# One piece of w_in over two DMA queues, the first scores in other PSUM banks, and other counts of filler products, in a recurrent-attention and shrink kernel

## The chip, the core and the metric

The kernel runs on one core of one Trainium2 chip. The metric is the time of one execution on the device in microseconds (us), as a median over executions. The core has a matrix engine (PE, with its weight loads shown as PEld), a vector engine (DVE), a scalar engine (ACT), a general engine (POOL), and a sync engine (SP) that here only issues DMA transfers. ACT can issue transfers too. Every engine works through its own list of instructions strictly in the order in which they were written; engines meet through semaphores only.

## The reference

Four batches, eight heads, 768 steps, head size 48. A state of 48 x 48 per head decays and is updated at each step, and the attention's output feeds a two-layer block with the activation h - tanh(h):

```
for t in range(S):
    state = alpha[:, :, t, :, None] * state + einsum('bhd,bhe->bhde', k[:, :, t], v[:, :, t])
    y[:, :, t] = einsum('bhd,bhde->bhe', q[:, :, t], state)
x = y.transpose(0, 2, 1, 3).reshape(3072, 384)
h = x @ w_in                      # 384 x 2048
out = (h - tanh(h)) @ w_out       # 2048 x 384
```

The weights arrive as 64-bit floats, all else as 32-bit floats.

## The kernel before

**Tiling.** The 3072 tokens are worked in 12 units (u) of 256, each of two chunks (c) of 128. For each unit the recurrence is done in chunk form: alpha, k and q are turned so that head dimensions lie on partitions, running products of alpha are made by scans forwards (`W`) and backwards (`U`), k and q are scaled with them (`kT`, `qT`), a product of the two gives the scores of a chunk, these are masked (`pm`), and the output y is the masked scores times v plus q times the state. The result `xT` goes through 8 steps (s) of the two-layer block: `first u:s` (six products with w_in, line 1080), `square` and `quad` on ACT (lines 1089 and 1093), `cube` and `shrunk` on DVE (1097 and 1101), `second u:s` (products with w_out, line 1125 for units 0 and 1, line 1146 after them).

**Weights.** w_in and w_out come in eight pieces each, `in0` to `in7` and `out0` to `out7`. A piece is fetched by `load_weight` (lines 39 to 44): a piece of w_in as eight transfers of 96 KB (six of 48 rows, two of 16), a piece of w_out as one. All are issued by SP. Each is then read by two ACT instructions (lines 86 and 87) and finished by two on DVE (lines 89 and 90). There are four raw buffers, so the fetch of a piece waits until the piece four before it was read.

**The start.** For unit 0, alpha, k, q and v are loaded in two halves each, one half issued by SP and one by ACT (lines 584 and 595). PE turns them by products with an identity matrix (`turn`, line 663): alpha's two parities a and b into the PSUM banks `o0` and `o1`, k's into the two `h` banks, q's into the large tile `sc`. ACT and DVE copy alpha out (line 670). DVE then makes U and W for each chunk and multiplies k and q out of PSUM (line 679). The scores of chunk 0 stand in tile `sc` as well, those of chunk 1 in the `h` banks (lines 782 to 800). `sc` exists once, so the scores of chunk 0 can only be written when all four multiplications of q have read it. Then come `masked` (819), `back` (925, k turned back), `natural` (930, its copy by ACT), `update` (938), `state` (953, 955), `gaps` (830, 833, small copies by ACT), `y` (850 to 860) and `x` (911, 920: ACT copies y into `xT`). `first 0:0` needs `x` of both chunks and in0 finished.

**The order.** A planner (class `Planner`) holds tasks with an engine, an estimated duration, dependences and a latency, lists them by an estimated schedule, and the program is written in that order. Its estimates set only the order of instructions on the engines; nothing waits for them on the chip. Two of its settings matter here. `plan.begin` is when it thinks that an engine starts. `plan.filler` puts products of the identity with itself (`spin`, line 1208) into PE's list, one for every 0.35 us of a gap that the plan leaves on PE before `y 0.0`; nobody reads their result. The filler is written into PE's list, so PE works it off whether or not there is a gap.

**DMA semaphores.** Transfers take eight semaphores in turn, in the program's order across both issuing engines. The program's instructions show the consequence: every issue from the ninth on first waits until the transfer that last held its semaphore has landed. While it waits, nothing behind it on its engine runs.

Of the kernel before, what the change touches and what calls it, by code (L numbers as in the profile page):

```python
# [9 lines left out]
FP32 = mybir.dt.float32  # L10
# [7 lines left out]
P = 128  # L18
# [17 lines left out]
R_MAX = 2.0 ** 60  # L36


def load_weight(nc, pool, rows, **kw):

    raw = pool.tile([P, WN], I64 if rows[0][2].dtype != FP32 else FP32, name="raw", **kw)
    for at, js, src in rows:
        nc.sync.dma_start(out=raw[at].rearrange("p (j n) -> p j n", n=src.shape[-1])[:, js], in_=src)
    return raw


# [275 lines left out]
class Planner:  # L322
# [64 lines left out]
    def order(self):  # L387
        names = {t[0]: i for i, t in enumerate(self.tasks)}
        assert len(names) == len(self.tasks)
        before, after = ([[] for _ in self.tasks] for _ in range(2))  # L390
        for i, t in enumerate(self.tasks):
            edges = {names[a]: self.tasks[names[a]][6] for a in t[4]}
            if t[7]:
                edges.setdefault(names[t[7]], 0.0 if self.tasks[names[t[7]]][1] == t[1] else 0.25)
            for j, lat in edges.items():
                before[i].append((j, lat))
                after[j].append((i, lat))
        chance = random.Random(self.SEED)
# [12 lines left out]
        plan = sorted(((starts[i], n, self.tasks[i][5], i) for n, i in enumerate(order)), key=lambda x: x[:2])  # L411

        engine, until, us, do = self.filler
        filled, free = [], self.begin.get(engine, 0.0)
        for x in plan:
            name, e, length = self.tasks[x[3]][:3]
            if e == engine and until:
                filled += [(free, -1, do, None)] * int(max(0.0, x[0] - free) / us)
                free = x[0] + length
                until = until if name != until else None  # L420
            filled.append(x)
        return filled


def fast(tc, q, k, v, alpha, moe_w_in, moe_w_out, out, w_in, w_out, ident, ok, pad_rows):
    nc = tc.nc
    B, H, S, D = q.shape
    NP = H // 2
# [9 lines left out]
    PLAIN = 2  # L438
# [4 lines left out]
    with ExitStack() as ctx:  # L443
# [23 lines left out]
        def by_matmul(u, what):  # L467
            return u < len(TURNED) and what in TURNED[u]
# [80 lines left out]
        raw_of = {}  # L549

        def fetch(what, s):
            raw_of[what, s] = load_weight(nc, raw_pool, weight_parts(moe_w_in, moe_w_out, pad_rows, what, s), bufs=4)

        def convert(what, s):
            it = []
# [7 lines left out]
        for n, (what, s) in enumerate(pieces):  # L563
            rank = RANK[what] + 2 * s
            held = pieces[n - 4] if n >= 4 else None
            add(f"fetch {what}{s}", "SP", 5.7 if n < 2 else 4.3 if what == "in" else 2.0, rank - 30, [held and f"read {held[0]}{held[1]}"],
                lambda what=what, s=s: fetch(what, s), lat=2.5)
# [35 lines left out]
        def gla(u, rank):  # L603
# [17 lines left out]
            for what, name in enumerate(("aT", "kT", "qT", "v")):  # L621
                go(f"load {name}", "SP", 1.3 if direct or what == 3 or by_matmul(u, what) else 2.2, -9 + 0.1 * what,
                   [what < 3 and u > 0 and not by_matmul(u - 1, what) and not by_matmul(u, what) and f"{name}{prev}"]
                   + [u == 1 and ("kUba 0" if what == 3 else "turn qTb 0")]
                   + [f"{last} {u - 2}.{CU - 1}" for last in ("y", "state") if what == 3 and u > 1
                      and (last == "y" or (u - 2) % UPB < UPB - 1)],
                   lambda what=what: load(u, what), lat=2.9 if u == 0 else 3.6 if u < PLAIN else 4.5)

            def widen(what):
                for hh in range(2):  # L630
# [51 lines left out]
            for n, ab in enumerate("ab"):  # L682
# [87 lines left out]
            def chunk(c):  # L770
# [11 lines left out]
                def scores():  # L782
                    if c == 0:

                        xT[u] = two.tile([P, NP, TU], FP32, name="xT")
                    if u == 0 and c == 1:
                        sc = m["sc", c] = [ps_h.tile([P, 2, TU], FP32, name="h").rearrange(
                            "p a t -> p (a t)").rearrange("p (g t) -> p g t", t=P) for _ in range(2)]
# [25 lines left out]
                def masked():  # L814
                    sc = m["sc", c]
                    if direct:
                        m["pm", c] = [two.tile([P, NP, P], FP32, name=f"pm{r}", tag=tag) for r, tag in enumerate("zw")]
                        for r, to in enumerate(m["pm", c]):
                            V.tensor_mul(to, sc[r] if c else sc[:, r], mask.unsqueeze(1).to_broadcast([P, NP, P]))
# [384 lines left out]
        def spin():  # L1204
# [1 line left out]
            if not spun:  # L1206
                spun.append(ps_o.tile([P, P], FP32, name="spin", tag="o2"))
            T.matmul(spun[0], lhsT=ident, rhs=ident, start=True, stop=True)  # L1208
# [113 lines left out]
```

## Time and profile before

| what | value |
|---|---|
| four executions | 575.84, 576.33, 580.06, 576.11 us |
| median | 576.22 us |
| the profiled execution's own time | 575.63 us |
| its span, first to last instruction | 573.9 us (1.73 us lie around it) |
| mean granted PE clock | 0.995 |
| PE, DVE, ACT busy | 98%, 79%, 56% |
| instructions | 13746 |

The page of the profile gives, for each engine, its busy time and count; PE's count has two entries for each 32-bit product, and one for each transpose. A busy PE is not yet a PE at its peak, because a product's end is modelled. What counts in the following is therefore the distance from the start of one group of products to the start of the next. A timeline row has the start, the length and the engine, then source line, operation, tiles and count; in square brackets stands the idle time just before it and what ended it. A table by windows gives the busy time of each engine in a stretch, the PE clock that was granted (1.00 is full), the share of the DMA engines in use and GB/s.

Where PE's first 55 us go, by the starts of its groups in the timeline: fillers from 1.57, alpha's turning from 5.39, the other turnings to 10.78, fillers, `back` and `update` to 14.1, nothing to 16.36, scores from 16.36, y from 20.87, the turnings of unit 1 from 25.60, `first 0:0` from 28.32, `y 1.1` up to 54.28. From 54.28 on `first` and `second` follow each other at 2.59 and 2.58 us, then 2.59 and 2.27.

### The profile page before, as it was taken

The numbers are of one execution on the slowest core, as the hardware profiler recorded it, in microseconds if no ns is written. First come the engines' busy times: TensorE is split into PE (matmuls) and PEld (weight loads), VectorE is DVE, ScalarE is ACT, GpSimd is POOL, SyncE is SP. The second block draws the span as 40 slices with busy tenths as digits, with TensorE's granted clock in tenths as the row PEclk, the third lists the DMA queues.
The fourth block names the chain that finished last, engine by engine and source line by source line (L and its number), as shares of the span: only waits on it lengthen the run. The fifth ranks groups of instructions, "written<-read, shape, count | busy, mean of one in ns | idle before, by whom it ended". The sixth has DMA issues, their size and how long they took to land.

```text
span 573.9 us, 13746 instructions
## 1 busy us (share of the span) xinstructions
PE 563.1 (98%) x5583; PEld 497.7 (87%) x5583; DVE 450.7 (79%) x886; ACT 323.4 (56%) x559; POOL 4.8 (1%) x22
## 2 busy tenths in 40 slices
PE   8899999999999999999999999999999999999995
PEld 8777777778999989998998999899898999899995
DVE  6888889999999996896895895896797745544643
ACT  3699895647687775676584374364353433333530
POOL 3000000000000000000000000000000000000000
PEclk9899999999999999999999999999999999999999
DMA  8889871335664762562630320310200000000001
GB/s 179 206 243 249 263 155 52 88 85 137 113 136 132 148 138 89 122 135 76 180 112 8 81 60 2 85 53 10 57 8 1 30 7 3 29 8 0 29 1 35
DMA packets 60713, 50.84 MB, mean 89 GB/s; under 512 B 35776, under 2 KB 50400, under 8 KB 60640
## 3 DMA queue, kind: packets, MB, share of 16 engines
q1 hardware_dynamic: 57728, 48.88, 34.1%
q10 hardware_dynamic: 2912, 0.98, 0.8%
q8 instruction: 46, 0.75, 0.6%
q14 instruction: 27, 0.22, 0.1%
HBM read 44.04 MB, written 4.72 MB: 85 GB/s over the span
## 4 chain that ended last, share of the span: by engine, by line
PE 95%; DVE 2%; DMA 1%; issue 0%; ACT 0%; POOL 0%; DVEq 0%; POOLq 0%
PE h L1080 43%; PE o L1146 33%; PE o L1125 7%; PE sc L805 2%; PE sc L878 2%; PE sc L888 2%; PE sc L811 2%; PE sc L991 1%; DMA raw<-in_moe_w_out_dram 1%; PE spin L1208 1%; PE turned L663 1%; DVE W L730 0%; PE y L853 0%; PE h L795 0%; PE y L860 0%
## 5 line engine op out<-in xcount | busy, mean ns | idle before, releaser
L1080 PE MATMUL h<-xT,w_in 128*128 128x256 f32 x1152 | 265.1, 380 | 0.6 <-DVE w_in L90 0.6
L1080 PEld LDWEIGHTS h<-xT,w_in 128*128 128x128 f32 x1152 | 215.4, 190 | 28.0 <-DVE w_in L90 0.7
L1089 ACT ACTIVATE u<-h 128x512 f32<-128x512 f32 x96 | 57.0, 594 | 179.1 <-PE h L1080 178.6
L1097 DVE TENSOR_TENSOR w<-h,u 128x512 f32<-128x512 f32 x96 | 65.7, 685 | 79.2 <-ACT u L1089 78.8
L1146 PE MATMUL o<-b,e 128*128 128x192 f32 x480 | 90.9, 326 | 0.0
L1146 PE MATMUL o<-w_out,e 128*128 128x192 f32 x320 | 81.4, 337 | 0.0
L1146 PEld LDWEIGHTS o<-b,e 128*128 128x128 f32 x480 | 80.2, 190 | 0.0
L1101 DVE SCALAR_TENSOR_TENSOR g<-z,w 128x512 f32<-128x512 f32 x96 | 65.3, 681 | 4.0 <-PE o L1125 1.2
L1146 PE MATMUL o<-b,g 128*128 128x192 f32 x320 | 65.1, 326 | 0.0
L1093 ACT ACTIVATE z<-u 128x512 f32<-128x512 f32 x96 | 60.4, 629 | 2.6
L1146 PEld LDWEIGHTS o<-w_out,e 128*128 128x128 f32 x320 | 55.7, 189 | 4.4
L1146 PEld LDWEIGHTS o<-b,g 128*128 128x128 f32 x320 | 54.2, 190 | 0.0
L1107 ACT ACTIVATE big<-u 128x1024 f32<-128x1024 f32 x48 | 50.4, 1050 | 0.0
L1125 PE MATMUL o<-w_out,g 128*128 128x384 f32 x128 | 44.0, 488 | 0.0
L1125 PEld LDWEIGHTS o<-w_out,g 128*128 128x128 f32 x128 | 24.1, 190 | 13.7
L1113 DVE TENSOR_TENSOR e<-g 128x256 f32<-128x256 f32 x80 | 33.3, 417 | 1.8
L1114 DVE TENSOR_TENSOR e<-g 128x256 f32<-128x256 f32 x80 | 33.2, 415 | 0.0
L639 DVE STREAM_TRANSPOSE aT<-ar 128x256 f32<-128x256 f32 x44 | 28.3, 644 | 2.8 <-ACT ar L633 1.7
L730 DVE TENSOR_TENSOR_SCAN W<-aT,before 128x1032 f32<-128x1032 f32 (+1 forms) x13 | 27.7, 2128 | 0.0
L711 DVE TENSOR_TENSOR_SCAN U<-aT,after 128x1032 f32<-128x1032 f32 (+1 forms) x13 | 27.6, 2128 | 0.1
L1115 DVE TENSOR_TENSOR e<-g 128x128 f32<-128x128 f32 x80 | 22.5, 282 | 0.0
L639 DVE STREAM_TRANSPOSE qT<-qr 128x256 f32<-128x256 f32 x40 | 20.5, 628 | 0.0
(141 smaller groups left out, 555.1 us busy)
## 6 DMA issues: line engine op xcount, KB each, us to landing
raw<-in_moe_w_out_dram SPq DMA_DIRECT2D x16, 768.0 KB, 4.9
raw<-in_moe_w_in_dram SPq DMA_DIRECT2D x80, 96.0 KB, 4.6
raw<-in_moe_w_in_dram SPq DMA_DIRECT2D x16, 288.0 KB, 5.0
vt<-in_v_dram SPq DMA_DIRECT2D x23, 192.0 KB, 4.0
ar<-in_alpha_dram SPq DMA_DIRECT2D x44, 96.0 KB, 2.6
kr<-in_k_dram SPq DMA_DIRECT2D x40, 96.0 KB, 2.9
qr<-in_q_dram SPq DMA_DIRECT2D x40, 96.0 KB, 2.2
out_dram<-cross SPq DMA_DIRECT2D x19, 96.0 KB, 1.7
```

The source lines that it names most:

```text
L639: V.transpose(to, raws[what][:, g, :, 0:32])
L730: V.tensor_tensor_scan(out=m["W"][:, ns].rearrange("p n t -> p (n t)"), data0=aT[:, a:z], data1=before[:, a:z], initial=0.0, op0=ALU.mult, ...
L1080: T.matmul(h[:, a, :], lhsT=w_in[:, j, f * P:(f + 1) * P], rhs=xT[u][:, j, :], start=(j == 0), stop=(j == KT - 1))
L1089: A.activation(m["u", s], m["h", s], AF.Square, scale=W_SCALE ** -1.5)
L1093: A.activation(m["z", s], m["u", s], AF.Square, bias=QB, scale=QA * W_SCALE)
L1097: V.tensor_mul(m["w", s], m["h", s], m["u", s])
L1101: V.scalar_tensor_tensor(out=g.rearrange("p a c t -> p (a c t)"), in0=m["z", s], scalar=QK, in1=m["w", s], op0=ALU.add, op1=ALU.mult)
L1107: A.activation(big, m["us", s // 2].rearrange("p s t -> p (s t)"), AF.Relu, bias=-U_FAST, scale=W_SCALE, accum_out=over[:, n:n + 1])
L1113: V.tensor_add(e[:, 0:2, :], g[:, 0], g[:, 1])
L1114: V.tensor_sub(e[:, 2:4, :], g[:, :, 1, :], g[:, :, 0, :])
L1125: T.matmul(m["o"][c], lhsT=g[:, a, c, :], rhs=w_out[:, f, :], start=(f == 0), stop=(f == FT - 1))
L1146: T.matmul(o[n][:, i], lhsT=g_, rhs=w_, start=(s_ == 0 and (n, i) in ((0, 0), (1, 0), (2, 1), (3, 0))), stop=(s_ == FS - 1), skip_group_ch ...
```

## The change

The diff, cut to its core:

```diff
-def load_weight(nc, pool, rows, **kw):
+def load_weight(nc, pool, rows, queues=None, **kw):
-    for at, js, src in rows:
-        nc.sync.dma_start(out=raw[at]..., in_=src)
+    for n, (at, js, src) in enumerate(rows):
+        (queues[n % len(queues)] if queues else nc.sync).dma_start(out=raw[at]..., in_=src)
...
-                filled += [(free, -1, do, None)] * int(max(0.0, x[0] - free) / us)
+                gap = x[0] - free
+                filled += [(free, -1, do, None)] * int(gap / (1.5 * us) if free == self.begin.get(engine) else (gap + 0.3) / us if gap > 0.2 else 0)
...
-            raw_of[what, s] = load_weight(nc, raw_pool, weight_parts(...), bufs=4)
+            raw_of[what, s] = load_weight(nc, raw_pool, weight_parts(...),
+                                          queues=[A, nc.sync] if (what, s) == pieces[0] else None, bufs=4)
...
-            add(f"fetch {what}{s}", "SP", 5.7 if n < 2 else 4.3 if what == "in" else 2.0, ...
+            add(f"fetch {what}{s}", "SP", 3.0 if n == 0 else 5.0 if n == 1 else 4.3 if what == "in" else 2.0, ...
...
-                   lambda what=what: load(u, what), lat=2.9 if u == 0 else 3.6 if u < PLAIN else 4.5)
+                   lambda what=what: load(u, what), lat=2.5 if u == 0 else 3.6 if u < PLAIN else 4.5)
...
-                       ["load qT", later and f"aT{ab}" if by_matmul(u, 0) else "masked 0.0"], lambda n=n: turn(2, n))
+                       ["load qT"] + [later and f"qW{x}{y} 0" for x in "ab" for y in "ab"], lambda n=n: turn(2, n))
...
-                    if u == 0 and c == 1:
-                        sc = m["sc", c] = [ps_h.tile([P, 2, TU], FP32, name="h")... for _ in range(2)]
+                    if u == 0:
+                        sc = m["sc", c] = [(ps_h if c else ps_o).tile([P, NP, P], FP32, name="scores", tag="h" if c else f"o{r}")
+                                           for r in range(2)]
...
-                            V.tensor_mul(to, sc[r] if c else sc[:, r], mask...)
+                            V.tensor_mul(to, sc[r], mask...)
...
-        plan.filler = "PE", "y 0.0", 0.35, spin
-        plan.begin.update(SP=0.8, PE=1.5, ACT=3.0, DVE=4.8)
+        plan.filler = "PE", "y 0.0", 0.24, spin
+        plan.begin.update(SP=0.8, PE=1.5, ACT=5.4, DVE=4.8)
```

Of in0's eight transfers four now go to ACT's queue (three of 48 rows, one of 16) and four to SP's. The scores of chunk 0 stand in alpha's banks `o0` and `o1`. The number of fillers goes from 19 (10, 3, 3, 3) to 28 (8, 4, 5, 5, 6).

The planner's other estimates move instructions on every engine. The lists of the two built programs stand against each other so (PE, from its first instruction on; numbers are unit.chunk or unit:step):

```
PE before: 10 spin, turn alpha a b, k a, q a, k b, q b, 3 spin, back 0.0, 3 spin, update 0.0, 3 spin,
  scores 0.0, back 0.1, scores 0.1, update 0.1, y 0.0, y 0.1, turn k a, k b, q a of unit 1,
  first 0:0, first 0:1, turn q b, back 1, first 0:2, scores 1.0, first 0:3, y 1.0, second 0:0, scores 1.1,
  first 0:4, second 0:1, y 1.1, first 0:5, second 0:2, first 0:6, ...
PE after:  8 spin, turn alpha a b, 4 spin, q a, k a, k b, q b, back 0.0, 5 spin, update 0.0, 5 spin,
  scores 0.0, 6 spin, scores 0.1, back 0.1, y 0.0, y 0.1, update 0.1, first 0:0, turn k a, q a, k b, q b,
  first 0:1, back 1, first 0:2, scores 1.0, first 0:3, second 0:0, y 1.0, scores 1.1, second 0:1,
  first 0:4, first 0:5, y 1.1, second 0:2, first 0:6, ...
SP before: 4 loads, in0 (8), alpha of unit 1 (4), in1 (8), k (2), q (2), in2 (8), v (2), in3 (8), out0, ...
SP after:  4 loads, in0 (4), alpha of unit 1 (4), in1 (8), in2 (8), k (2), q (2), v (2), in3 (8), out0, ...
ACT before: 4 loads, alpha a, gaps 0.0, size U, natural 0.0, state 0.0, read in0, gaps 0.1, natural 0.1,
  size W, widen alpha of unit 1, x 0.0, read in1, x 0.1, ...
ACT after:  4 loads, alpha a, in0 (4 issues), gaps 0.0, natural 0.0, read in0, state 0.0, size U,
  widen alpha of unit 1, size W, gaps 0.1, natural 0.1, read in1, x 0.0, x 0.1, ...
DVE before: alpha b, U a, U b, kT a with U a (2), ends a, W a, ends b, qT a (2), W b, kT b and qT b (4), ...
DVE after:  alpha b, U a, kT a with U a (2), ends a, W a, U b, qT a, ends b, qT a, W b, kT b and qT b (4), ...
```

From `second 0:3` on PE's list is, but for one place (`back` of unit 2 stands one `second` earlier), the same in both; on DVE, ACT and SP neighbours are exchanged in units 0 to 4 and in a few places after them. ACT's four issues of in0 wait, in this order, for the landing of: SP's half of v; SP's second and third transfers of in0; the first transfer of alpha for unit 1.

More of the change, by code (lines that the diff above doesn't have):

```diff
@@ L36 @@
 R_MAX = 2.0 ** 60
-def load_weight(nc, pool, rows, **kw):
+def load_weight(nc, pool, rows, queues=None, **kw):
     raw = pool.tile([P, WN], I64 if rows[0][2].dtype != FP32 else FP32, name="raw", **kw)
-    for at, js, src in rows:
-        nc.sync.dma_start(out=raw[at].rearrange("p (j n) -> p j n", n=src.shape[-1])[:, js], in_=src)
+    for n, (at, js, src) in enumerate(rows):
+        (queues[n % len(queues)] if queues else nc.sync).dma_start(out=raw[at].rearrange("p (j n) -> p j n", n=src.shape[-1])[:, js], in_=src)
     return raw
@@ L551, in fetch @@
         def fetch(what, s):
-            raw_of[what, s] = load_weight(nc, raw_pool, weight_parts(moe_w_in, moe_w_out, pad_rows, what, s), bufs=4)
+            raw_of[what, s] = load_weight(nc, raw_pool, weight_parts(moe_w_in, moe_w_out, pad_rows, what, s),
+                                          queues=[A, nc.sync] if (what, s) == pieces[0] else None, bufs=4)
         def convert(what, s):
@@ L565, in fast @@
             held = pieces[n - 4] if n >= 4 else None
-            add(f"fetch {what}{s}", "SP", 5.7 if n < 2 else 4.3 if what == "in" else 2.0, rank - 30, [held and f"read {held[0]}{held[1]}"],
+            add(f"fetch {what}{s}", "SP", 3.0 if n == 0 else 5.0 if n == 1 else 4.3 if what == "in" else 2.0, rank - 30, [held and f"read {held[0]}{held[1]}"],
                 lambda what=what, s=s: fetch(what, s), lat=2.5)
@@ L785, in scores @@
                         xT[u] = two.tile([P, NP, TU], FP32, name="xT")
-                    if u == 0 and c == 1:
-                        sc = m["sc", c] = [ps_h.tile([P, 2, TU], FP32, name="h").rearrange(
-                            "p a t -> p (a t)").rearrange("p (g t) -> p g t", t=P) for _ in range(2)]
+                    if u == 0:
+                        sc = m["sc", c] = [(ps_h if c else ps_o).tile([P, NP, P], FP32, name="scores", tag="h" if c else f"o{r}")
+                                           for r in range(2)]
                     else:
@@ L818, in masked @@
                         for r, to in enumerate(m["pm", c]):
-                            V.tensor_mul(to, sc[r] if c else sc[:, r], mask.unsqueeze(1).to_broadcast([P, NP, P]))
+                            V.tensor_mul(to, sc[r], mask.unsqueeze(1).to_broadcast([P, NP, P]))
                         return
```

## The prediction

> **What bounds the kernel now.** I read the page's busy times first, then the table by windows, then the timelines of PE, ACT and SP.
>
> ```profile
> PE 563.1 (98%) x5583; PEld 497.7 (87%) x5583; DVE 450.7 (79%) x886; ACT 323.4 (56%) x559; POOL 4.8 (1%) x22
> ...
> PE 95%; DVE 2%; DMA 1%; issue 0%; ACT 0%; POOL 0%; DVEq 0%; POOLq 0%
> ```
>
> PE is the bound, and 95% of the chain that ended last. From 54.28 us its groups follow each other without a hole. I summed what they take there beyond 2.59, 2.58 and 2.27 us each: 8.3 us by the end, in 0.1 to 0.2 us pieces, none over 0.3. So a gain can only come from the start, and one made there stays only if PE stays full behind it. The next rows are the start's.
>
> ```profile
> 1.57 3.89 PE L1208 MATMUL spin<-ident 128*128 128x128 f32 x20 [1.57 <-POOL ident masks.py:199]
> 5.39 2.84 PE L663 MATMUL turned<-ident,rough 128*64 128x128 f32 x48
> ...
> 13.41 0.94 PE L1208 MATMUL spin<-ident 128*128 128x128 f32 x6
> 16.36 1.16 PE L795 MATMUL sc<-qT,kT 48*128 48x128 f32 x16 [2.00 <-DVE qT L679]
> 17.45 0.60 PE L925 MATMUL y<-ident,kT 112*128 112x112 f32 x4
> 17.98 1.95 PE L795 MATMUL h<-qT,kT 48*128 48x128 f32 x16
> 19.86 1.09 PE L938 MATMUL y<-vt,kn 128*64 128x48 f32 x16
> ...
> 25.60 1.92 PE L663 MATMUL turned<-ident,rough 128*64 128x128 f32 x32
> ```
>
> Alpha's slower half, on ACT's queue, landed at 4.33 (0.81 plus 3.5), yet its turning began at 5.39, behind the fillers. The first scores waited 2.00 us for DVE's last multiplication of q.
>
> ```profile
> 15.00:16.00 1.00, 0.00 (x0) 0.00 (x0) 1.00 (x5) 1.00 (x2) 0.00 (x0) 1.00 0.59 197
> 16.00:17.00 1.00, 0.65 (x10) 0.65 (x12) 0.37 (x2) 0.76 (x3) 0.00 (x0) 1.00 0.66 207
> 17.00:18.00 1.00, 1.00 (x16) 0.74 (x12) 0.44 (x1) 0.00 (x0) 0.00 (x0) 1.00 0.74 207
> 18.00:19.00 1.00, 1.00 (x11) 1.00 (x12) 1.00 (x3) 0.92 (x2) 0.00 (x0) 0.58 0.71 225
> 19.00:20.00 1.00, 1.00 (x14) 0.78 (x11) 0.86 (x2) 0.97 (x3) 0.00 (x0) 0.50 0.72 150
> 20.00:21.00 1.00, 1.00 (x18) 0.91 (x20) 1.00 (x3) 0.93 (x2) 0.00 (x0) 0.50 1.14 253
> ```
>
> The column behind POOL is the granted clock: after PE's idle stretch it is 0.50 for 3.4 us (18.2 to 21.6). The last rows are ACT's and SP's.
>
> ```profile
> 9.35 0.27 ACT L830 COPY v_gap<-vt 128x96 f32<-128x96 f32 x1 [2.11 <-DMA vt<-in_v_dram]
> ...
> 14.53 1.08 ACT L86 ACTIVATE more<-raw 128x768 int16<-128x768 uint32 x1 [0.67 <-DMA ar<-in_alpha_dram]
> ...
> 4.35 7.91 SPq L43 DMA_DIRECT2D raw<-in_moe_w_in_dram  x8
> ```
>
> SP's eight issues of in0 start at 4.35, 4.74, 5.87, 6.22, 7.72, 8.08, 10.34 and 10.71: every other one as the load that last held its semaphore lands (the halves on ACT's queue of alpha, k, q and v, at 4.33, 5.85, 7.71 and 10.32; v's other half at 9.27). In0 was whole at 14.4 (10.71 plus 3.7), when ACT read it.
>
> **The change, part by part.** I keep a ledger of PE time that does no needed work, up to `first 0:2`.
>
> *Before.* Fillers 1.57 to 5.39: 3.82. Nine later ones: 0.82 + 0.79 + 0.66 = 2.27. Wait for the scores, 14.08 to 16.36: 2.28. Half clock: the second scores 1.88 against 1.09 for the first, `update` 1.02 against 0.59, the first v_gap group 1.10 against 0.78: 1.54. Wait of `first 0:3` for in3, at 40.10: 1.22 where the same group takes 0.55 later: 0.67. Sum 10.58.
>
> *Fillers in front.* Filler entries come every 0.213 us up to 4.51, then every 0.112. Sixteen instead of twenty save four at 0.112 = 0.45, or 0.85 should the clock rise later. Alpha starts at 4.94: 3.37 stays. Alpha has landed, so nothing is late.
>
> *Twenty fillers behind.* 40 entries at 0.112 plus four switches of 0.15: 5.1 us, 2.8 more than the nine. They would cost that if PE did not otherwise wait. PE: alpha to 6.69, four fillers to 7.74; q's half landed at 7.71 (1.92 plus 5.8), so no wait. Four turnings (0.87 each, the last 0.97) end at 11.3, `back` 11.75, five fillers 13.0, `update` 13.6, five fillers 14.87.
>
> *Scores in alpha's banks.* They now need qT a only. DVE: alpha copy at 7.03, U a 7.83 (0.80 behind it, as before). k a, now turned behind q, is out of PE at 9.5; the turnings' consumers start 1.2 us behind a group's start: 9.82 and, for k b's, 10.7. W a at 11.02, U b 1.13 later, q a's multiplications at 13.29 and 13.99, ends at 14.39. Scores can go at 14.45; PE reaches them at 14.87. So the 2.28 wait is gone, and fillers decide. Chunk 1's multiplications end at 16.84; six fillers (1.5) end at 17.45. Nothing waits for alpha's banks: both copies are over at 7.72.
>
> *The half clock.* PE has no hole over 0.4 us from 4.94 to 23.5, so I take the 1.54 as gone. Its other end: all of it stays.
>
> *in0 over two queues.* ACT's four issues are held until v (9.27), SP's second and third in0 transfers (10.54 and 10.78, same places as before) and alpha's first transfer for unit 1 (issued 7.72, in the place of one that landed at 11.42). The last goes at 11.5 and, by 2.4 to 3.0 us to landing on the quiet queue of 14 to 18 us, lands about 14.2: in0 gains 0.2, not half its 7.91. The issues cost ACT nothing it has to do: behind them stand `gaps` (12.0) and `natural` 0.0 (12.25 to 12.78); `back` is out at 12.1, and `update` 0.0, which PE reaches at 13.0, needs it. Each us more shows at once.
>
> *ACT behind it.* In order, by rows of before: in0 1.85 from 14.3, state 0.32, size U 1.25, widening 1.26, size W 1.25, two small copies 0.4, `natural` 0.53, in1 1.85, x 0.0 0.48: free at 23.5. PE: scores 0.0 to 15.96, fillers 17.45, scores 0.1 18.55, `back` 19.1, y 0.0 20.7 (0.78 + 0.79), y 0.1 23.5 (0.58 + 0.78 + 0.78 + 0.69), `update` 24.1. x 0.1 runs 23.9 to 24.5, so `first 0:0` stands still 0.45. Before, the same set of work ended at 25.60.
>
> *Later.* SP finishes in1 near 16.0 (before 17.87); in2 now precedes unit 1's k and q, which go at 19.8 instead of 17.99 and land by 27 (25.09 plus 1.8). PE wants q at 27.8. in3 is whole about 30.5 instead of 34.9, which takes the 0.67. DVE reaches `cube 0:0` 0.2 late for `first 0:2`: 0.2. Then PE leads DVE by more: DVE is busy for 19.74 of the 24 us from 66 to 90 and 48.59 of the 50 to 140, so 5.7 us are idle. A lead of 1.5 needs 1.5 of them, and DVE's own list is early as well: nothing lost; the other end is the whole 1.5.
>
> *After:* 3.37 + 5.1 + 0.45 + 0.2 = 9.12. Gain 10.58 - 9.12 = 1.46, say **1.5 us**. Against the profiled execution's own 575.63 that gives 574.1; against the median 576.22, 0.59 above it, **574.7**.
>
> [...] Four issues of 0.42 would bring in0 to 12.7; the row has issues held by landings, and I go by it.
>
> **Rivals.**
>
> *No gain: the clock still falls, or DVE takes it at 90 to 140 us.* For: 28 fillers may not lie where PE waits, and DVE is 97% busy there. Against: no hole over 0.45 us, and the 5.7 idle. Either gives the 1.5 back: 576.2.
>
> *Everything clears, and the later 0.2 us holes shrink.* No stall of 0.45 or 0.2, fillers in front worth 0.85 instead of 0.45: 1.46 + 0.65 + 0.4 = 2.5; with a tenth of the 8.3 us of small holes, as units 0 to 4 are reordered, 3.3: 572.9.
>
> *Slower: ACT's queue stands in the issues.* One place: the fourth issue, which waits for alpha of unit 1. For: nothing on ACT passes it, and `natural` 0.0, in0's reading and so `first 0:0` stand behind it. By the slowest landing of the start (7.84 us, v on ACT's queue) it goes at 7.72 + 7.84 = 15.6 instead of 11.5: 4.1 later, in0 4.1 later, and the gain of 1.5 turns into a loss of 2.6. PE then stands some 4 us in front of `update` 0.0, longer than in the hole that halved its clock before, and pays the 1.54 again: 576.2 + 2.6 + 1.5 = 580.3. It decides from 1.5 us late on, that is from 13.0. Against: the transfer that had that place took 3.7.
>
> **How the numbers follow.** Likeliest, 0.61: a gain of 0.3 to 2.7, at 574.7, own range 573.5 to 575.9. No gain: 0.16. Everything clears: 0.10, nearly all (0.09) past 0.5% (2.9 us, about what a measurement of this kernel tells from no change). Slower: 0.13, of which 0.10 past 0.5%. To both ends I move some of the likeliest, because units 0 to 4 are reordered on DVE, and a hole of 1 us or two more or less would not show in this sum: 0.06 to faster, 0.04 to slower. That gives faster 0.09 + 0.06 = 0.15, slower 0.10 + 0.04 = 0.14, same 0.71. The range, 572.6 to 577.8, leaves the worse end of the slow case out, and the best end of the clear one.
>
> **What would show it.** Alpha's turning at 4.9; scores at 14.9 without a wait; a clock of 1.00 from 4.5 on; in0 read near 14.3; `first 0:0` at 24.5; `y 1.1` over near 55 with one `first` more behind it than before. Wrong if ACT's first read of in0 starts after 16, if the clock falls again, or if holes over 0.3 us appear between 60 and 180.

## The result, and the profile after

| | before | after |
|---|---|---|
| median | 576.15 us (78 runs) | 577.93 us (52 runs) |
| range | 575.37 to 580.06 | 576.68 to 582.23 |
| profiled execution, its span | 575.63, 573.9 | 578.6, 576.6 |
| mean granted clock | 0.995 | 0.998 |
| `first 0:6` starts, in the profile | 59.55 | 62.39 |

The ratio after to before is 1.0023, 95% interval 1.0014 to 1.0031: 1.3 us slower. (The means of all executions give 1.0023 too; the medians lie further apart, 1.8 us, because 24 of before's 78 executions lie some 2.5 us above the rest and raise its mean.) The forecast was 574.7, range 572.6 to 577.8. The two profiled executions lie 3.0 us apart, as before's is 0.5 below its median and after's 0.7 above its own; so what follows from the two profiles shows more than the typical loss.

The page of after, the lines for busy time and for the chain that ended last:

```profile
PE 565.4 (98%) x5601; PEld 499.6 (87%) x5601; DVE 451.0 (78%) x886; ACT 321.5 (56%) x559; POOL 4.8 (1%) x22
...
PE 89%; DMA 5%; SPq 3%; ACT 1%; issue 1%; DVE 0%; ACTq 0%; DVEq 0%
```

PE is still the bound, but 11% of the chain is now other work, where it was 5%. PE's timeline (start, length, engine, line, operation, tiles, count, idle before and what ended it):

```profile
1.57 3.78 PE L1212 MATMUL spin<-ident 128*128 128x128 f32 x16 [1.57 <-POOL ident masks.py:199]
5.28 3.12 PE L666 MATMUL turned<-ident,rough 128*64 128x128 f32 x32
...
16.63 1.16 PE L799 MATMUL scores<-qT,kT 48*128 48x128 f32 x16
17.72 1.60 PE L1212 MATMUL spin<-ident 128*128 128x128 f32 x12
...
23.82 0.85 PE L857 MATMUL y<-pm,v_gap 128*32 128x128 f32 x12 [0.71 <-ACT v_gap L834]
...
26.88 3.03 PE L1084 MATMUL h<-xT,w_in 128*128 128x256 f32 x12 [0.20 <-ACT xT L924]
...
36.95 2.77 PE L1084 MATMUL h<-xT,w_in 128*128 128x256 f32 x12
...
41.55 2.83 PE L1084 MATMUL h<-xT,w_in 128*128 128x256 f32 x12 [0.77 <-DVE w L1101]
...
51.58 0.59 PE L1084 MATMUL h<-xT,w_in 128*128 128x256 f32 x2
53.67 5.01 PE L1084 MATMUL h<-xT,w_in 128*128 128x256 f32 x22 [1.49 <-DVE w_in L90]
...
62.39 2.75 PE L1084 MATMUL h<-xT,w_in 128*128 128x256 f32 x12
```

Of the last five rows the first is `first 0:2`, the next `first 0:3`, then `first 0:4` in two parts (with `first 0:5` behind it), and `first 0:6`. The same four in the timeline of before (0:2, 0:3, 0:4, 0:6):

```profile
35.60 2.83 PE L1080 MATMUL h<-xT,w_in 128*128 128x256 f32 x12
...
40.10 2.86 PE L1080 MATMUL h<-xT,w_in 128*128 128x256 f32 x12 [0.60 <-DVE w_in L90]
...
47.82 2.86 PE L1080 MATMUL h<-xT,w_in 128*128 128x256 f32 x12
...
59.55 2.75 PE L1080 MATMUL h<-xT,w_in 128*128 128x256 f32 x12
```

But for the fillers, what PE has done by `first 0:6` is the same in both kernels, and from there to the end of the span it is 514.4 us before and 514.2 after. So all of the loss lies ahead of it, and the start of `first 0:6` is the ledger for every profile below. The scores go without a wait, and the granted clock stays at 1.00 behind the start (after the columns of PE, PEld, DVE, ACT and POOL stands the clock):

```profile
14.00:18.00 4.00, 4.00 (x52) 3.58 (x51) 3.96 (x10) 0.68 (x3) 0.00 (x0) 1.00 0.61 163
18.00:22.00 4.00, 4.00 (x50) 3.42 (x51) 3.35 (x9) 3.95 (x7) 0.00 (x0) 1.00 0.85 214
```

But alpha's turning (the second row of PE's timeline) starts at 5.28 and lasts 3.04 us. Its entries come every 0.21 us up to 7.7 and every 0.11 from there, as before's fillers do at 4.51, so I read this as a clock that rose only at 7.7. (The clock's column prints 1.00 ahead of both points too; the pace is what shows it.) And `first 0:4` (51.58) stops after its first product for 1.49 us, until DVE has converted a piece of w_in. ACT's timeline:

```profile
9.79 4.07 ACTq L43 DMA_DIRECT2D raw<-in_moe_w_in_dram  x4
13.91 0.27 ACT L834 COPY v_gap<-vt 128x96 f32<-128x96 f32 x1 [5.92 <-DMA raw<-in_moe_w_in_dram]
...
17.94 1.09 ACT L86 ACTIVATE more<-raw 128x768 int16<-128x768 uint32 x1 [3.33 <-DMA raw<-in_moe_w_in_dram]
```

ACT stands in its four issues from 9.79 to 13.87, and in0 is whole at 17.8 instead of 14.4.

### The profile page after: what moved, and what is told of

It is laid out like the page before. It is cut to its first block, busy times and chain, and to the rows that moved or that the text cites. A ratio compares the mean times of both kernels' runs of the same rounds, so it can differ in the third digit from the quotient of the medians.

```text
span 576.6 us, 13783 instructions
## 1 busy us (share of the span) xinstructions
PE 565.4 (98%) x5601; PEld 499.6 (87%) x5601; DVE 451.0 (78%) x886; ACT 321.5 (56%) x559; POOL 4.8 (1%) x22
## 4 chain that ended last, share of the span: by engine, by line
PE 89%; DMA 5%; SPq 3%; ACT 1%; issue 1%; DVE 0%; ACTq 0%; DVEq 0%
PE h L1084 42%; PE o L1150 32%; PE o L1129 6%; DMA raw<-in_moe_w_out_dram 2%; PE sc L809 2%; PE sc L882 2%; SPq L43 2%; PE sc L892 2%; PE sc L815 2%; DMA vt<-in_v_dram 1%; PE sc L995 1%; DMA ar<-in_alpha_dram 1%; DMA raw<-in_moe_w_in_dram 1%; SPq L598 0%; ACTq L598 0%
## 5 line engine op out<-in xcount | busy, mean ns | idle before, releaser
L1150 PEld LDWEIGHTS o<-b,g 128*128 128x128 f32 x320 | 54.2, 190 | 0.0
L86 ACT ACTIVATE more<-raw 128x768 int16<-128x768 uint32 x16 | 17.3, 1083 | 8.8 <-DMA raw<-in_moe_w_in_dram 6.3
```

The lines of the kernel that those rows point to most:

```text
L1150: T.matmul(o[n][:, i], lhsT=g_, rhs=w_, start=(s_ == 0 and (n, i) in ((0, 0), (1, 0), (2, 1), (3, 0))), stop=(s_ == FS - 1), skip_group_ch ...
```

## The experiments

Medians are of 8 to 12 runs, each group of kernels with 23 to 35 runs of before beside it (medians 576.03 to 576.36); R is the ratio to before with its 95% interval.

**The four parts apart.** T is the theory that the split costs, R1 that the new order does, R2 that the added fillers do.

`e1_all_on_sp`, after with in0 on SP:

```diff
-                                          queues=[A, nc.sync] if (what, s) == pieces[0] else None, bufs=4)
+                                          queues=None, bufs=4)
```

> The changed kernel with in0's eight transfers all on SP's queue again; order, banks and fillers as changed. Theory T (ACT stands in its four issues, the last of them is late, and in0 lands at 17.8 instead of 14.4): in0 lands near 14.5 again, ACT's first read of it starts there and not at 17.9, the 0.7 to 1.0 us wait for v_gap in front of y 0.1 is gone, first 0:0 starts 1.5 to 2.5 us earlier than 26.9; time 574.9 to 576.0, that is 1.5 to 2.5 below the changed kernel's 577.5 and not above before's 576.15. Rival R1 (the order is what costs) and rival R2 (the 2.8 us of added fillers cost): in0 earlier, but the time stays at 577.0 to 578.0.

577.53 us, R 1.0023 (0.9998 to 1.0047): no better than after. In0 landed at 14.9 and `first 0:0` started at 25.12, as T expects, but it then stood 0.76 us behind its first product, waiting for a conversion. In the profiles `first 0:2` comes 0.9 earlier than in after; the medians are 0.4 apart, too little to tell. T falls as the main cause.

`e3_banks_alone`, before with

```diff
-                    if u == 0 and c == 1:
-                        sc = m["sc", c] = [ps_h.tile([P, 2, TU], FP32, name="h")... for _ in range(2)]
+                    if u == 0:
+                        sc = m["sc", c] = [(ps_h if c else ps_o).tile([P, NP, P], ..., tag="h" if c else f"o{r}") for r in range(2)]
```

> The kernel before with one part of the change alone: chunk 0's first scores in alpha's banks. Instruction order as before. By the prediction's term the 2.0 us wait of the first scores for DVE's last multiplication of q goes or shrinks, as far as DVE is ready (it was at 14.45 against 16.36). Theory T and R1, R2 alike: scores start up to 1.5 us earlier, but first 0:0 hangs on ACT's x 0.1 behind v_gap and in0, so at most 1 us of it reaches the end: 575.2 to 576.2. If the scores' wait was itself the bound of the start: 574.2 to 575.0. If it changes nothing because q's multiplications end last either way: 576.0 to 576.3.

575.44 us, R 0.9973 (0.9954 to 0.9992). PE's timeline:

```profile
14.99 1.16 PE L795 MATMUL scores<-qT,kT 48*128 48x128 f32 x16 [0.41 <-DVE qT L679]
...
25.58 0.70 PE L1080 MATMUL h<-xT,w_in 128*128 128x256 f32 x2
27.23 1.99 PE L1080 MATMUL h<-xT,w_in 128*128 128x256 f32 x8 [0.95 <-DVE w_in L90]
```

The wait for the scores shrank from 2.00 to 0.41, the clock stayed up, `first 0:6` came at 58.03. So this part of the change is a gain of 0.9 us in the median, and here too a `first` stops behind its first product for a conversion.

`e4_old_fillers`, after with before's filler rule:

```diff
-                filled += [...] * int(gap / (1.5 * us) if free == self.begin.get(engine) else (gap + 0.3) / us if gap > 0.2 else 0)
+                filled += [...] * int(max(0.0, gap) / us)
-        plan.filler = "PE", "y 0.0", 0.24, spin
+        plan.filler = "PE", "y 0.0", 0.35, spin
```

> The changed kernel with before's rule for fillers (and 0.35 us for each), so fewer products behind alpha's turning; split, banks and order as changed. R2 (fillers cost what they last where PE does not wait): 1 to 2 us faster than the changed kernel, 575.5 to 576.5. Theory T and R1: PE reaches update 0.0 and the scores earlier and waits there instead, for ACT's in0, v_gap and x, so the time stays within 0.5 of the changed kernel's (577.0 to 578.0), or rises by up to 1.5 where the clock halves in the holes.

578.64 us, R 1.0018 (0.9995 to 1.0040), not faster than after: in the profiled execution PE stood 1.74 us for `natural` 0.0 behind ACT's issues, and then ran at half clock from 15.3 to 25.6. Even its fastest execution (576.67) is above what R2 expects: R2 falls.

`e5_order_alone`, after with e1's and e4's edits, and chunk 0's scores where before had them:

```diff
-                    if u == 0:
+                    if u == 0 and c == 1:
```

> The changed kernel's task order (its planner's estimates and waits) with before's banks and before's rule for fillers, in0 all on SP: the order alone. R1 (the order costs: in2 before unit 1's k and q, the k-then-q turnings, ACT's and DVE's lists): 577.0 to 578.0, and the same late first 0:4 and 0:5 hole near 52 us and late out0 near 40. Theory T: 575.7 to 576.7, the order worth nothing by itself (within 0.5 of before).

581.25 us, R 1.0062 (1.0038 to 1.0086), worse than R1 expects. PE waited 2.58 us for the scores; the table by windows shows the clock:

```profile
15.00:17.00 2.00, 0.00 (x0) 0.00 (x0) 2.00 (x5) 2.00 (x4) 0.00 (x0) 0.81 0.68 188
17.00:19.00 2.00, 1.86 (x16) 1.78 (x16) 0.08 (x1) 1.95 (x4) 0.00 (x0) 0.50 0.80 206
...
25.00:27.00 2.00, 2.00 (x26) 1.49 (x24) 1.93 (x5) 1.53 (x3) 0.00 (x0) 0.63 1.20 259
```

Half clock from 16.2 to 26.5 us, ten us where before's profile had 3.4. So the order costs without split, banks and added fillers too, and here a long stretch of half clock goes with it.

**Which number makes the order.** In the list of the built program only two of the planner's numbers move anything: the durations of in0's and in1's fetch, and the latency 2.5 of unit 0's loads. (The traces agree: e7 and e12 below run the same instructions in the same order but for the fillers, and so do e11 and e1.) Theory O says that the durations cost, S that the split does.

```diff
 e6, e9 (after)   -3.0 if n == 0 else 5.0 if n == 1 else 4.3 ...   +5.7 if n < 2 else 4.3 ...
 e9 also          e1's edit (in0 on SP)
 e7 (e3)          -5.7 if n < 2 else 4.3 ...   +3.0 if n == 0 else 5.0 if n == 1 else 4.3 ...
 e8 (e3)          the new filler rule, and 0.24 for 0.35
```

> The changed kernel with one line of it undone: the planner's duration for fetching in0 and in1 is 5.7 us again instead of 3.0 and 5.0. In0 stays split over both queues, banks and filler rule as changed. So the order is nearly before's again (k a turned right behind alpha, masks before the first w_in, unit 1's turnings before first 0:0). Theory O (the order that follows from these two numbers is what costs, through DVE's list): masks of chunk 0 on DVE at 16.5 to 17.0 instead of 17.5, no hole over 0.6 us between 48 and 56; the work before first 0:6 is over by 59.0 to 60.5 instead of 62.4; time 575.0 to 576.5. Rival S (the split costs in itself): in0 still late, time 576.8 to 578.5. Rival R2 (the added fillers cost): 576.5 to 577.5.

576.41 us, R 1.0007 (0.9994 to 1.0020).

> As the changed kernel with the durations of 5.7 us, and in0's eight transfers all on SP's queue: beside the same kernel with the split it gives what the split is worth on a good order. Theory O: 574.8 to 576.0, within 0.7 of the one with the split. Rival S: 1.5 to 2.5 faster than the one with the split.

575.37 us, R 0.9984 (0.9966 to 1.0001). On one order the split costs 1.0 us in the median, though the intervals overlap. The row of `update` 0.0 in PE's timeline of e6 (its slowest execution, 578.56) suggests why:

```profile
16.01 1.04 PE L942 MATMUL y<-vt,kn 128*64 128x48 f32 x16 [2.18 <-ACT kn L934]
```

> The kernel before with chunk 0's first scores in alpha's banks and the changed planner durations for in0 and in1 (3.0 and 5.0 us), nothing else: the order that follows from these two numbers, without split and without added fillers. Theory O: 2 to 5 us slower than the same kernel with the durations of before (575.4): 577.5 to 580.5, with DVE idle behind k a's turning, and PE idle long enough in front of the scores to lose its clock in part of the executions. Rivals S and R2, by which the order is worth nothing: 575.0 to 576.0.

575.45 us, R 0.9988 (0.9969 to 1.0007): as e3. The durations alone cost nothing; theory O, as stated, falls.

> The kernel before with the first scores in alpha's banks and the changed filler rule (9 products in front of alpha's turning, 5, 5 and 5 behind it, where it was 10, 3, 3 and 3); order as before. By rows of the kernel with the banks alone, PE came to the scores at 14.3 and DVE let them go at 15.0; six more products at 0.25 us (two entries of 0.112 each) make PE come at 15.6 to 15.8, so they cost 0.6 to 0.8 in an execution that kept its clock and save up to 1.5 in one that lost it. Theory O: 575.0 to 576.0 median, with a narrower spread. R2 (fillers cost in full, 1.5): 576.5 to 577.0.

575.51 us, R 0.9994 (0.9972 to 1.0015): six more fillers behind alpha's turning, and one fewer in front, cost nothing measurable.

**Both numbers together.** O2 says that the order of both together costs, C that they are harmless. S1 and S2 are two reasons for the price of the split.

```diff
 e11 (e7)           -lat=2.9 if u == 0   +lat=2.5 if u == 0
 e12 (e1)           -lat=2.5 if u == 0   +lat=2.9 if u == 0
 e13 (e6)           -queues=[A, nc.sync]   +queues=[nc.gpsimd, nc.sync]
 e14 (e7)           -max(0.0, x[0] - free) / us   +max(0.0, x[0] - free) / (1.4 * us if free == self.begin.get(engine) else us)
```

> The kernel before with the first scores in alpha's banks, the changed durations for in0 and in1 (3.0 and 5.0 us), and now also the changed latency of unit 0's loads (2.5 for 2.9 us). In0 on SP, filler rule as before. Without that last number the kernel took 575.45. Theory O2 (what costs is the order that the two estimates give together: both w_out conversions on DVE ahead of in4's and in5's w_in, second 0:0 ahead of first 0:4): first 0:4 and 0:5 stand together again with a hole of 0.5 to 1.9 us, equal work (first 0:6) 1 us or more later than with one estimate, time 576.5 to 579.0. Rival C (the two estimates alone are harmless, and the changed kernel's loss comes from fillers and split together): 575.0 to 576.0.

579.06 us, R 1.0041 (1.0020 to 1.0061): one number more, and 3.6 us slower than e7. `first 0:4` in PE's timeline of e7, then in that of e11, and the table by windows of e11:

```profile
47.48 2.75 PE L1080 MATMUL h<-xT,w_in 128*128 128x256 f32 x12
```


```profile
50.40 0.59 PE L1080 MATMUL h<-xT,w_in 128*128 128x256 f32 x2
53.18 4.07 PE L1080 MATMUL h<-xT,w_in 128*128 128x256 f32 x11 [2.19 <-DVE w_in L90]
```

```profile
52.00:53.00 1.00, 0.00 (x0) 0.00 (x0) 0.86 (x2) 1.00 (x3) 0.00 (x0) 1.00 0.17 47
...
54.00:56.00 2.00, 2.00 (x7) 1.62 (x6) 1.83 (x5) 1.77 (x3) 0.00 (x0) 0.56 0.79 312
```

The two came to `first 0:2` within 0.2 us of each other (35.42 and 35.24). The stop of `first 0:4` is there, 2.19 us, and the clock falls behind it, for 3.4 us from 54.2.

> The changed kernel with in0 on SP alone and one further number undone: the latency of unit 0's loads 2.9 us again instead of 2.5. With 2.5 it took 577.53. Theory O2: first 0:4 and first 0:5 no longer stand together, no hole over 0.6 us between 48 and 56, 575.2 to 576.2. Rival C: 577.0 to 578.0 still.

576.93 us, R 0.9998 (0.9978 to 1.0017), between the two; C falls with e11 all the same. The stop at `first 0:4` was gone, but PE stood 1.39 us in another place (see e16). But for the fillers its list is that of e7, which took 575.45.

> As the changed kernel with the durations of 5.7 us (which took 576.41, against 575.37 with in0 on SP alone), but in0's second half goes over POOL's queue in place of ACT's. Theory S1 (the split costs because ACT's work stands behind the four waiting issues): update 0.0 no longer waits 2.5 us for natural, 575.0 to 575.8. Rival S2 (the split costs because in0's transfers come later or disturb others, whoever issues them): 576.2 to 577.0.

575.53 us, R 0.9970 (0.9949 to 0.9990), as S1 expects. In0's last transfer from POOL's queue landed at 13.8, ACT was free, and `update` 0.0 ran at 13.82 without a wait. Two things changed at once, though: POOL's four transfers had semaphores of their own and went between 5.57 and 7.19 without waiting for a landing, so in0 was early as well (13.8, against 18.1 in e6). What speaks for S1 is that in e6 nothing waited for in0's landing: ACT came to read it at 18.37, after it had landed.

> An attempt at a faster kernel: before, with the first scores in alpha's banks, the durations 3.0 and 5.0 for in0 and in1 and the latency of before (575.45), and seven products instead of ten in front of alpha's turning. Alpha had landed at 4.6 at the latest and its turning began at 5.6 to 6.1 there; with 14 filler entries at 0.112 to 0.213 us it can begin at 4.6 to 4.9, and DVE's list, which then waits for k a, moves with it: 0.5 to 1.0 faster, 574.4 to 575.0. If the clock rises later for it, or another wait takes its place: 575.2 to 576.0.

576.75 us, R 0.9999 (0.9981 to 1.0017), a miss. PE's timeline, and its groups from 60 to 100 us (count, busy and mean, idle before and releaser):

```profile
1.57 3.36 PE L1208 MATMUL spin<-ident 128*128 128x128 f32 x14 [1.57 <-POOL ident masks.py:199]
4.86 2.98 PE L663 MATMUL turned<-ident,rough 128*64 128x128 f32 x32
7.67 1.04 PE L663 MATMUL sc<-ident,rough 128*64 128x128 f32 x16
```

```profile
L1080 PE MATMUL h<-xT,w_in 128*128 128x256 f32 x80 | 18.6, 382 | 0.4 <-DVE w_in L90 0.4
L991 PE MATMUL sc<-ident,kT 112*128 112x112 f32 x8 | 1.0, 266 | 1.2 <-DVE kT L735 1.2
```

Alpha's turning began 0.42 earlier than in after with 16 entries and 0.75 earlier than in e3 with 20, but its entries came every 0.21 us up to 6.96, and it ended at 7.67 (in e3, with a turning of 1.80 from 5.61: at 7.41). And where PE was early, at 60 to 100 us, it waited 1.6 us for DVE.

**In the changed kernel itself.**

```diff
 e15 (after)        -RANK = {"in": -3, "out": 3}   +RANK = {"in": -3, "out": 4}
 e16                e12 unchanged
 e17 (e15)          -queues=[A, nc.sync]   +queues=[nc.gpsimd, nc.sync]
 e18 (e3)           in0 with queues=[nc.gpsimd, nc.sync]
```

> The changed kernel whole, with one number of the planner different: the rank of the w_out pieces is 4 instead of 3, so that DVE converts in4's w_in before out1's w_out, and one `first` stands between the two second products. Split, fillers, banks and estimates as changed. Theory O2 (the hole at first 0:4 and 0:5, behind both w_out conversions, is what costs): no hole over 0.6 us between 48 and 56, 1.0 to 1.9 us faster than the changed kernel, 575.8 to 576.7. If the loss lies in the start (split and fillers) alone: 577.2 to 578.0.

578.92 us, R 1.0043 (1.0025 to 1.0060). My expectation missed, and the miss gave the mechanism. DVE's conversions of in4 and in5, and `first 0:4` in PE's timeline:

```profile
46.50 0.96 DVE L90 CUSTOM_DVE_ANT_0 w_in<-bits,more 128x1536 uint16<-128x1536 uint16 x1 [0.17 <-DVE bits L89]
...
53.25 0.96 DVE L90 CUSTOM_DVE_ANT_0 w_in<-bits,more 128x1536 uint16<-128x1536 uint16 x1
```

```profile
52.15 0.59 PE L1084 MATMUL h<-xT,w_in 128*128 128x256 f32 x2
54.26 2.42 PE L1084 MATMUL h<-xT,w_in 128*128 128x256 f32 x10 [1.52 <-DVE w_in L90]
```

in4, the only piece that `first 0:4` reads, was done at 47.5. Its second product still waits, until in5 is done at 54.2.

> The same kernel as e12_old_lat_sp, once more: the changed kernel with in0 on SP and the latency of 2.9. If the 1.6 us stall of PE at 44.5 belongs to the kernel: there again, and the median stays at 576.5 to 577.3. If it was of one execution: gone, profiled execution near 575.3, and the median 575.3 to 576.3.

577.44 us, R 1.0016 (0.9995 to 1.0036): the stall is in both profiled executions, so it belongs to the kernel. PE's timeline, the row of `issue` being a wait for nothing that the profile shows:

```profile
44.12 0.62 PE L815 MATMUL sc<-vt,kn 64*48 64x48 f32 x29
46.65 0.29 PE L815 MATMUL sc<-vt,kn 64*64 64x48 f32 x3 [1.91 <-issue]
```

> As e15, and in0's second half over POOL's queue in place of ACT's: the changed kernel with both suspects mended. Order and split together as the cause: 574.8 to 575.6, under before's 576.2. If something else of the changed kernel costs: 576.0 to 577.0.

578.53 us, R 1.0031 (1.0012 to 1.0050): a miss like e15, with the same stop at `first 0:4` (1.52 us).

> An attempt at a kernel that beats both: before, with the first scores in alpha's banks (575.44) and in0's second half over POOL's queue. Order and fillers as before. In0 lands up to 0.6 us earlier and in1, k and q of unit 1 up to 1.2 us earlier, so the 1.3 us hole in first 0:0 (waiting for in1) shrinks: 574.5 to 575.3. If DVE's list is full from 60 to 180 us anyway and takes it back: 575.2 to 575.7.

575.33 us, R 0.9974 (0.9957 to 0.9991): faster than both kernels, not to be told from e3.

**The shared range.** In w_in's layout the columns of one piece are three stretches, one for each row block, and other pieces lie between them. In the built list the second product of `first` 0:0, 0:1 and 0:4 (row block 1) waits for DVE, and the conversions of in2, in3, in4 and in6 wait for PE. The edit gives every piece its own stretch:

```diff
-    w_in = consts.tile([P, KT, d_ff], FP32, name="w_in")
+    w_in = consts.tile([P, FT // 2, KT, 2 * P], FP32, name="w_in")
-                dst = w_in[:, :, 2 * s * P:2 * (s + 1) * P] if what == "in" else ...
+                dst = w_in[:, s] if what == "in" else ...
-                            T.matmul(h[:, a, :], lhsT=w_in[:, j, f * P:(f + 1) * P], ...
+                            T.matmul(h[:, a, :], lhsT=w_in[:, s, j, a * P:(a + 1) * P], ...
```

The lists of after and of e19 (after with this edit), `first 0:0`'s second product and in2's conversion:

```
after: Matmult h<-xT,w_in  waits DVE               w_in<-bits,more  waits DVE, PE, Activation
e19:   Matmult h<-xT,w_in                          w_in<-bits,more  waits DVE, Activation
```

Else the lists of PE, ACT and SP are the same.

> The changed kernel whole, with w_in laid out by pieces, (piece, row block, column) instead of (row block, column), so that no product of first 0:n and no conversion of another piece share a range. Instructions and their order as in the changed kernel; the second product of each first no longer waits for DVE, and DVE's conversions no longer for PE. Theory O3 (first 0:4 stands until in5 is converted, and first 0:0 until in1 is, though neither reads them; in3's conversion stands 1.7 us for first 0:2): the hole of 1.9 us at 51.8 and DVE's 1.7 us wait at 38 to 40 go, equal work (first 0:6) comes 1.5 to 2.5 us earlier, time 575.2 to 576.5. Rival (DVE reaches in4's and in5's conversion late anyway and PE waits at another product): 577.0 to 578.0.

576.43 us, R 0.9991 (0.9968 to 1.0014), where after had 1.0023 (1.0014 to 1.0031). PE's timeline, `first 0:3`, `first 0:4` with `0:5`, and `first 0:6`:

```profile
40.51 2.86 PE L1084 MATMUL h<-xT,w_in 128*128 128x256 f32 x12
...
50.57 5.34 PE L1084 MATMUL h<-xT,w_in 128*128 128x256 f32 x24
...
59.62 2.75 PE L1084 MATMUL h<-xT,w_in 128*128 128x256 f32 x12
```

Both stops are gone, and DVE's wait in front of in3's conversion too; it was this in after:

```profile
39.84 0.96 DVE L90 CUSTOM_DVE_ANT_0 w_in<-bits,more 128x1536 uint16<-128x1536 uint16 x1 [1.70 <-PE h L1084]
```

`first 0:6` comes 2.77 us earlier, 2.56 of it behind the start of `first 0:2` (36.74 against 36.95). Alpha's turning ended 0.84 earlier in this execution, but nothing of that was left at `first 0:0` (26.85 against 26.88). In the medians, measured apart, the gain is 1.5, and the two intervals just touch. O3 holds: the stops are seen to go, and the time with them.

`e20_best`, e18 with the same edit:

> An attempt at a kernel that beats both: before, with the first scores in alpha's banks, in0's second half over POOL's queue, and w_in laid out by pieces. Without the layout it took 575.33; its 1.3 us hole behind the first product of first 0:0 should go, 0.5 to 1.5 faster: 573.8 to 574.9. If DVE's full list from 100 to 180 us takes it back: 575.0 to 575.6.

575.29 us, R 0.9983 (0.9964 to 1.0001): no more than e18. PE came to `first 0:6` at 58.18, but waited 1.1 us between 55 and 100 us for conversions. None of the kernels tried went below the 575.3 to 575.5 of e3, e7, e8, e9, e13, e18 and e20.

## Why the prediction was wrong

The prediction had after 0.79 us ahead at the start of `first 0:2` (its gain of 1.46, less the wait of 0.67 for in3, which lies behind that point although the ledger is said to end there). In the profiles after was 1.35 behind there, so 2.14 were missed. From there to `first 0:6` it had the 0.67 gained; 1.49 were lost (25.44 us instead of 23.95), so 2.16 were missed. The miss has two halves, and the first two steps below are them.

**The step that failed: "Later", with its "nothing lost".** The two lists showed that `first 0:4` and `first 0:5` move together and that DVE's order changes. I priced a late `cube` at 0.2 and all else at nothing, and took the wait in front of `first 0:3` (0.67) as gone. It measured 0.84 (1.39 against 0.55), and the stop in `first 0:4` 1.66 (1.87 from its second entry to its third, where 0.21 is usual). The reason is a dependence that I did not look for: a `first` waits not only for its own piece, but also for the last conversion of w_in that was written before it. Before, in5's conversion was written behind `first 0:4`; the two estimates together (e11 against e7) put it in front. e19 takes the dependence away and the stops go. I read the order of tasks and never asked the built list what each of them waits for.

**In the start: "in0 over two queues" and "ACT behind it".** In0 was expected at 14.2 and landed at 17.8. The fourth issue went at 12.9, not 11.5, because the transfer that it waits for took 5.1 us instead of the 3.7 taken over from before, and its own took 4.9 instead of 2.4 to 3.0, beside alpha's four transfers of unit 1 (issued from 7.75 on, 4.2 to 5.2 us to landing), which the split had let ahead. ACT's first read of in0 at 17.94 was past the 16 that I had named as the refutation. From there ACT worked without a pause up to x 0.1, and `first 0:0` started at 26.88 instead of 24.5. "The issues cost ACT nothing" failed too: ACT stood in them until 13.87, and `natural` 0.0 went at 14.09 instead of 12.25. On the order of e6 and e9 the split costs 1.0, and over POOL's queue (e13) nothing that the runs show. In the changed kernel little of it reaches the end: without it (e1), `first 0:0` starts 1.76 earlier, but then waits for in1's conversion, the dependence of "Later" again. So the rival "ACT's queue stands in the issues" was the right mechanism at a place where it did not decide; its 13.0 was nearly met, its 580.3 not. Nor did the split save issue time: ACT's four issues stood 4.1 us, and in0's last issue went at 12.9 where before's went at 10.71.

**"Fillers in front".** Expected 0.45 to 0.85. Measured: alpha's turning began 0.1 earlier than before (5.28), and lasted 3.04 instead of 1.80. A late clock does not make the saved fillers worth more, as I wrote; it makes the turning itself run at half pace. e14 shows the same with fewer. That it came so late in this profile looks like chance and not like an effect of the fillers: the pace doubled between 4.51 and 7.38 in the five profiles with 20 entries in front, between 5.08 and 7.67 in the eleven with 16, and at 5.56 and 4.67 in two executions of one kernel (e12, e16); before's is the earliest of the 20, after's the latest. As e19 shows, this delay did not reach `first 0:0`.

**"The half clock": right in the profile, but no gain in the median.** The clock stayed at 1.00 behind 7.7 us. But before did not pay for the half clock as the ledger says. Over the five groups of runs, its 66 executions with a mean granted clock of 0.998 or more, which leaves no room for such a stretch, took 576.0 us on average, and the 35 at 0.994 or 0.995, as in its profile, 575.9. Only those at 0.990 to 0.993 (39 executions, 578.6) and below (10, 579.7) are longer (nine at 0.996 and 0.997 are left out). Whether a late rise of the clock or another wait takes the 1.54 back in the first kind, no run shows; the sum took all of it as gained.

The stretches between two changes of the clock were whole multiples of 3.41 us long in the profiles that show both ends: 13.65 and 3.41 in before (4.51 to 18.16 to 21.57, the first read from PE's pace), 10.25 in e4 (15.32 to 25.57), 10.24 in e5 (16.24 to 26.48), 3.41 in e11 (54.23 to 57.64). Of the last 3.41 us ahead of the fall at 18.16 in before, PE was idle for 1.61 and busy for 1.80.

**"Twenty fillers behind"** was right in length (5.16 against 5.1), and e8 shows that they cost nothing on before's order. On the two other orders the answer differs: e1 is 1.5 faster than e11, which lacks them, with intervals that overlap; e12 and e16 are 1.5 and 2.0 slower than e7, which lacks them, again with intervals that overlap, and their profiles show a stall of 1.4 and 1.9 us that is told of at the end.

**"Scores in alpha's banks"** was right. The scores went without a wait, 1.8 us later than said, because alpha was late. e3 shows that the banks alone, with before's order, give most of the gain that I had put on the whole change: 0.9 of 1.5.

No run puts all of this together in the changed kernel; e19, which mends "Later" alone, gives back 1.5 of the 3.2 us between forecast and measured median.

## What to carry to other kernels

Before pricing a new order, list what each moved instruction waits for in the built program: a write to one part of a tile can hold a read of another part, if the range of the one spans the other, and then the order in which they are written decides, not the data (in after `first 0:4` stopped 1.49 us for it, in e19 not at all). Do not issue a transfer from an engine that has work behind it, if issues wait for earlier landings (in after ACT stood 4.1 us in four of them); in e13 POOL's queue, whose issues waited for no landing, gave the same transfers at no cost that shows. A planner's estimate that differs by 0.4 us can move instructions on every engine (e7 to e11); change one at a time. Before counting a stretch of the one profiled execution as a gain, see whether the executions without it are faster at all.

## What was not expected of the hardware

- PE stood 1.4 us (e12) and 1.9 us (e16) behind the 29th of 32 products of one group, with no releaser. In both, a 16 KB packet on an instruction queue of the DMA had started 1.1 and 0.8 us before the group stopped. e7 has the same order there, fewer fillers ahead, such a packet at 43.9 too, and no stall. What PE waited for in e12 and e16, no run shows.
- The clock stayed at half for 3.4 us in before, and for ten in e4 and e5, though PE was busy without a hole for most of these ten. No run shows what holds it there, or what makes it fall. The five falls while PE had work came in or behind a stop of PE: of 2.00 us in before, 1.74 in e4, 2.58 in e5, 2.18 in e6, 2.19 in e11. But behind the stop of 1.49 us at 53.67 in after the granted clock was 1.00, and with the stop of 1.91 us in e16 the mean granted clock was 0.998, as in after.
- A gain in the first 60 us does not always last: e8, e13, e14 and e20 came to `first 0:6` at 58.2 to 59.0, and took 515.1 to 516.2 us from there instead of 514.4, with PE waiting for DVE for part of it (0.3 us in e8, 1.6 in e14) between 60 and 100 us; e3, at 58.03, took 514.3. Which orders lose there was not settled.
